# Row numbers cast once per batch, scatters behind a one-element GpSimd copy, z doubled by GpSimd, reciprocals taken in the expert tiles

## The chip, the core and the metric

The kernel runs on one core of one Trainium2 chip. The metric is the device time of one launch in microseconds (us). The profile is one execution recorded by the hardware profiler. Five engines work side by side: PE is TensorE (its weight loads are listed as PEld), DVE is VectorE, ACT is ScalarE, POOL is GpSimd, and SP is SyncE, which here only issues DMAs. GpSimd issues DMAs too, among them all indirect ones: a scatter that sends each of 128 rows to an address of its own.

## The reference

Two parts follow each other. The first is an attention without softmax that multiplies its result with u; the second is a dense feed-forward block to which each row adds the block of one expert out of eight, weighted with the softmax probability of that expert.

```python
# u, v: [8, 2816, 256]; z: [8, 2816, 64]
scores = (1.0 / S) * np.matmul(z, z.transpose(0, 2, 1))
attn = np.maximum(scores, 0.0) ** 2
x = (u * np.matmul(attn, v)).reshape(22528, 256)

y_dense = np.maximum(x @ w1_dense, 0.0) @ w2_dense        # 256 -> 512 -> 256
logits = x @ w_gate                                        # [22528, 8]
expert_idx = np.argmax(logits, axis=1)
gate_w = softmax(logits)[arange(N), expert_idx]
for e in range(8):
    mask = expert_idx == e
    y_moe[mask] = gate_w[mask, None] * (np.maximum(x[mask] @ w1[e], 0.0) @ w2[e])
return y_dense + y_moe
```

Since the largest logit is subtracted before the exponential, the chosen expert's probability is one divided by the sum of the exponentials. That is the only reciprocal in the kernel.

## The kernel before, in words

**Two stages.** The attention works through 176 row blocks of 128 rows, 22 in each of 8 batches. As soon as some row blocks have their x, they are routed: each row is given a place in the part of its expert in a buffer `xs` in DRAM, and a *scatter* sends it there, 576 bytes with x in bf16, the gate weight and the token's number. The expert stage reads `xs` back in tiles of 256 rows of one expert (70 of them) and then in pairs of 128 rows (22 of them, the last two only if they are needed), and sends the results to the output with indirect DMAs.

**The attention.** Row blocks are taken in groups of 2, 4, 4, 4, 4 and 4 per batch. For a group the scores against all 22 key blocks are computed on TensorE (L371), put through a ReLU by ScalarE (L386) or VectorE (L388) and squared by ScalarE (L399) or VectorE (L401; in the first two groups GpSimd may do it) into one of three buffers `A`. Since the scores are symmetric, part of A comes from the group before last by DMA transposes (L434). The products of A and v (`av`, L530) take two row blocks at a time in two passes over the 22 key blocks. `gate_x` (L559) multiplies with u and writes x to `pays`, a ring of 22 row blocks in SBUF, whose two last columns in use are the gate weight (column P, as float32) and the token number (column P + 1). Scores of up to two groups ahead fill TensorE's time in between.

**z.** For each batch, z is loaded (`load_z`), doubled along its columns by a copy in two halves (`turn_z`, L113), and transposed by SyncE's DMAs (L116). This is done during the batch before: the halves are due 6 and 7 row blocks after the batch's start, and the first scores that need them are computed from its fifth group on (row block 14).

**Routing.** Batches of row blocks are routed together: fourteen of 11, then 8, 6, 4 and 4 (`sizes`, L43), the first sixteen of them during the attention. `logits` (L587) multiplies with the gate's weights; `route_a` finds the largest logit, the exponentials `ex` and the one-hot `oh` of the chosen expert; `route_pre` counts on TensorE; the three parts of `route_b` write the gate weight (`se`, L634) and the token number (L635) to `pays` and work out the place of each row, a float32 number in `pos`. A batch is ready for scatters five row blocks and more after its last x.

**Scatters.** One is due at each *tick*, which comes once per row block (some 2.6 to 3.3 us). From row block 154 on, a second one is due in the middle of each pass. The last twelve are issued in the expert stage, one in each fifth slot (L1092 to L1095), with a `pause` behind it: a copy on GpSimd whose result is not read (L902). `scatter` casts one column of `pos` to an integer on VectorE (L675) and issues the indirect DMA on GpSimd (L677).

**What sets the order.** L67 gives a written order to four engines:

```python
    ctx.enter_context(tc.manual_schedule(engines={ET.PE, ET.Activation, ET.DVE, ET.SP}))
```

What is written first on one of these is issued first. A small planner makes this order while the kernel is built: work for VectorE or ScalarE is offered with a readiness time, a rank and an estimated duration per engine (`offer`), and `best` gives the engine that is free first the work that is ready first; TensorE's clock `now` is advanced by an estimate per piece of work (`pe`). The scatters are offered to VectorE with 0.1 us, because of their cast, and so are loads that are kept back by a small VectorE write (`soon`, rank 3; `turn_z` with 0.4 us). The routing's parts are offered with 1.3 us (`route_a`) and 0.8 us each (`chain`). GpSimd is not among the four: the framework that builds the program orders its instructions itself, within what their operands allow.

**The expert stage.** A slot computes, on TensorE, the dense block's first product, the second half's output of the tile two before, the expert's first product (L889) and the first half's output of the tile before (L897). VectorE copies the next tile's expert weights (L877). In `half` ScalarE copies the dense result out (L912), VectorE adds the expert's result times the row's gate weight (L913, the scalar `me[:, j, 0:1]` read back from `xs`), and GpSimd sends the 128 rows to the output (L915), with a `pause` behind every other one. `tokens` hands `half` the token numbers that came back with the rows.

## Time and profile before

| what | value |
|---|---|
| median of 3 runs | 939.89 us (938.05 to 944.79) |
| the profiled execution's own time | 936.83 us |
| its span | 934.7 us |
| mean granted TensorE clock | 0.99 |
| TensorE (PE) busy | 879.7 us, 94% |
| weight loads (PEld) busy | 762.7 us, 82% |
| VectorE (DVE) busy | 703.7 us, 75% |
| ScalarE (ACT) busy | 741.7 us, 79% |
| GpSimd (POOL) busy | 476.7 us, 51% |
| DMA | 127.64 MB, of these 61.54 MB read from HBM and 37.16 MB written |
| scatters to `xs` (L677) | 176, 199.2 us on GpSimd, mean 1132 ns |

The span runs from the first to the last recorded instruction. A busy time is the sum of an engine's recorded instructions; TensorE's matmuls are pipelined, so their ends are modelled. In the views that follow, `L677` is line 677 of the kernel, `xs<-pays,pi` names what an instruction writes and reads, and a time in brackets is the idle time of the engine ahead of an instruction with what ended it: `<-DVE pi L675` is an instruction of another engine, `<-issue` means that the profile shows nothing it waited for, and `<-remote` a release that the profile can't place. In the tables by stretches the engines stand in the order PE, PEld, DVE, ACT, POOL. A line of the waits reads: engine, tile and line that waited, what it waited for, total us, number of times, and the longest.

### The profile page before, as it was taken

What the parts mean: (1) busy time and instruction counts of PE and PEld (TensorE: products, weight loads), DVE (VectorE), ACT (ScalarE), POOL (GpSimd) and SP (SyncE); (2) the same over time, 40 slices, a digit from 0 to 9 for tenths busy, and PEclk for the clock granted to TensorE, in tenths of its full rate; (3) what the DMA queues carried; (4) which work ended last, traced back from release to release, by engine and by line L of the source; (5) the groups of instructions that cost most, each with busy time, mean ns of one, the idle gap of its engine ahead of it and who ended that gap; (6) DMA issues with size and microseconds to landing.
All of it is one profiled execution on the core that took longest, in us unless ns stands there. A gap on an engine that the chain in (4) does not pass through costs nothing.

```text
span 934.7 us, 30580 instructions
## 1 busy us (share of the span) xinstructions
PE 879.7 (94%) x12265; PEld 762.7 (82%) x12265; DVE 703.7 (75%) x1324; ACT 741.7 (79%) x916; POOL 476.7 (51%) x517
## 2 busy tenths in 40 slices
PE   7899999999999999999999988999999999999996
PEld 5788888888898898888888765878888888888775
DVE  7999988999898999999999873655654454446553
ACT  7999988999998999989989860666766676766664
POOL 2202342434344354344346334578877787876455
PEclk9999999999999999999999988999999999999999
DMA  7795896997997997997997845455544444443332
GB/s 146 119 177 124 150 177 134 158 195 147 157 191 152 172 196 142 177 198 139 182 181 150 132 105 88 108 120 114 119 111 112 109 113 109 117 103 95 85 88 70
DMA packets 257871, 127.64 MB, mean 137 GB/s; under 512 B 225470, under 2 KB 232894, under 8 KB 257728
## 3 DMA queue, kind: packets, MB, share of 16 engines
q1 hardware_dynamic: 230112, 70.24, 44.3%
q0 software_dynamic: 27616, 55.44, 27.8%
q8 instruction: 96, 1.57, 0.7%
q14 instruction: 47, 0.39, 0.2%
HBM read 61.54 MB, written 37.16 MB: 106 GB/s over the span
## 4 chain that ended last, share of the span: by engine, by line
PE 75%; issue 7%; DVE 5%; POOL 4%; ACT 4%; DMA 3%; another core or an unknown queue 1%; SPq 1%; POOLq 0%; DVEq 0%; ACTq 0%
PE o L530 38%; PE yy L897 13%; PE h_ps L889 12%; PE s L371 9%; POOL out_dram L915 3%; ACT A L399 2%; ACT r L386 1%; PE lg L587 1%; DVE A L401 1%; DMA xT<-pays 1%; DMA vb<-in_v_dram 1%; DVE ring L913 1%; DVE r L388 1%; ACT ring L912 1%
## 5 line engine op out<-in xcount | busy, mean ns | idle before, releaser
L530 PE MATMUL o<-vb,A 64*128 64x256 bf16 x7744 | 498.7, 271 | 12.3 <-issue 5.7
L530 PEld LDWEIGHTS <-A 64*128 64x128 bf16 x7744 | 411.1, 95 | 66.3 <-issue 12.4
L677 POOL DMA_INDIRECT xs<-pays,pi x176 | 199.2, 1132 | 274.3 <-DVE pi L675 224.9
L386 ACT ACTIVATE r<-s 128x1024 f32<-128x1024 f32 (+1 forms) x275 | 272.6, 1017 | 37.0 <-PE s L371 18.5
L399 ACT ACTIVATE A<-r 128x1024 bf16<-128x1024 f32 (+1 forms) x258 | 263.9, 1049 | 1.8 <-DVE vb L128 0.6
L892 ACT ACTIVATE ring<-h_ps 128x1024 bf16<-128x1024 f32 x180 | 185.6, 1032 | 95.1 <-PE yy L897 43.3
L401 DVE TENSOR_TENSOR A<-r 128x1024 bf16<-128x1024 f32 (+1 forms) x173 | 209.3, 1222 | 0.9
L913 DVE SCALAR_TENSOR_TENSOR ring<-yy,me,ring 128x256 f32<-128x256 f32 x180 | 86.3, 482 | 148.5 <-ACT ring L912 86.0
L388 DVE TENSOR_SCALAR r<-s 128x1024 f32<-128x1024 f32 x157 | 188.8, 1208 | 12.0 <-PE s L371 7.9
L915 POOL DMA_INDIRECT out_dram<-ring,me x140 | 145.9, 1042 | 63.7 <-DVE ring L913 34.2
L897 PEld LDWEIGHTS <-ring 128*128 128x128 bf16 x1440 | 140.0, 98 | 37.5 <-issue 21.4
L371 PE MATMUL s<-zT 64*128 64x512 bf16 (+1 forms) x944 | 159.4, 358 | 8.8 <-remote 3.8
L897 PE MATMUL yy<-w2d,ring 128*128 128x256 bf16 x720 | 107.9, 272 | 17.0 <-DVE ring L913 16.7
L897 PE MATMUL yy<-ring 128*128 128x256 bf16 x720 | 108.0, 273 | 0.0
L889 PE MATMUL h_ps<-ring 128*128 128x256 bf16 (+1 forms) x880 | 94.9, 253 | 1.7 <-issue 1.1
L889 PE MATMUL h_ps<-ring,w1d 128*128 128x256 bf16 x720 | 93.6, 273 | 2.6 <-ACT ring L892 1.2
L877 DVE COPY ring<-wall 128x2048 bf16 x110 | 81.9, 760 | 11.3 <-issue 8.4
L912 ACT COPY ring<-yy 128x256 f32<-128x256 f32 x180 | 68.1, 379 | 25.9 <-PE yy L897 12.2
L889 PEld LDWEIGHTS <-ring 128*128 128x128 bf16 x880 | 73.8, 98 | 11.4 <-DVE ring L877 2.3
L371 PEld LDWEIGHTS <-zT 64*128 64x128 bf16 x944 | 58.9, 94 | 25.3 <-issue 15.9
L889 PEld LDWEIGHTS <-w1d 128*128 128x128 bf16 x720 | 70.2, 98 | 11.3 <-issue 3.2
L559 DVE TENSOR_TENSOR pays<-o,ut 128x512 bf16<-128x512 f32 x88 | 60.7, 690 | 24.4 <-PE o L530 16.4
(118 smaller groups left out, 348.4 us busy)
## 6 DMA issues: line engine op xcount, KB each, us to landing
ut<-in_u_dram SPq DMA_DIRECT2D x88, 256.0 KB
vb<-in_v_dram POOLq DMA_DIRECT2D x16, 384.0 KB
vb<-in_v_dram POOLq DMA_DIRECT2D x16, 320.0 KB
wall<-in_moe_w_dram POOLq DMA_DIRECT2D x16, 256.0 KB
xs<-pays,pi POOLq DMA_INDIRECT x176
zr<-in_z_dram POOLq DMA_DIRECT2D x7, 352.0 KB
out_dram<-ring,me POOLq DMA_INDIRECT x140
A<-A SPq DMA_TRANSPOSE x128
```

What stands on the lines that cost most here:

```text
L371: nc.tensor.matmul(out=s[:, h, y * c:(y + 1) * c], lhsT=zT[r, k + h, :], rhs=zT[r, i0:i0 + w, :], start=True, stop=True)
L386: nc.scalar.activation(r[:, :, :c], s[:, :, :c], AF.Relu, scale=1.0 / S)
L388: nc.vector.tensor_scalar(out=r[:, :, :c], in0=s[:, :, :c], scalar1=1.0 / S, scalar2=0.0, op0=ALU.mult, op1=ALU.max)
L399: nc.scalar.activation(a, r, AF.Square)
L401: (nc.gpsimd if eng == "pool" else nc.vector).tensor_mul(a, r, r)
L530: nc.tensor.matmul(out=o[:, j, 0:D], lhsT=A[n][r, k, c:c + P], rhs=v_of[b][r, k, :], start=(p == 0 and x == 0), stop=(p == 1 and x == nK - 1))
L677: ins = nc.gpsimd.indirect_dma_start(out=xs, out_offset=bass.IndirectOffsetOnAxis(ap=pi[:], axis=0), in_=pays[:, g % (2 * G), 0:ROW].bitca ...
L889: nc.tensor.matmul(out=h_ps[:, f, hs, :], lhsT=w1(c, f), rhs=xT[:, hs, c, :], start=(c == 0), stop=(c == 1))
L892: nc.scalar.activation(h, h_ps[:].rearrange("p f h t -> p f (h t)"), AF.Relu)
L897: nc.tensor.matmul(out=y[:, k, :], lhsT=h[:, f, j * P:(j + 1) * P], rhs=w2(f), start=(f == 0), stop=(f == 3))
L913: nc.vector.scalar_tensor_tensor(out=ys, in0=y[:, 1, :], scalar=me[:, j, 0:1], in1=yd, op0=ALU.mult, op1=ALU.add)
L915: ins = nc.gpsimd.indirect_dma_start(out=out, out_offset=bass.IndirectOffsetOnAxis(ap=ids[j], axis=0), in_=ys, in_offset=None, bounds_chec ...
```

## The change

Six edits, of which the second and third belong together.

1. `turn_z`: the copy that doubles z is done by GpSimd and no longer by VectorE. It is no longer offered to the planner; it is written at its tick.
2. `route_b` part three casts the row numbers of a whole batch to integers at once (`pos`), and `scatter` hands a column of them to the indirect DMA. The 176 casts of one column each (L675) are gone.
3. A scatter is no longer offered to VectorE. At its tick a GpSimd copy of one element is written, from the piece of A that the planner gave last (`last_made`) to a one-element tile `pacer`, and the scatter behind it. The twelve scatters in the expert stage have no such copy.
4. The sum of the exponentials is written to `pays` as it is. The reciprocal is taken where the row comes back, in `tokens` of the expert stage: 128 x 2 numbers a tile (`mr`), which `half` uses as its scalar.
5. The token numbers are copied to `pays` by GpSimd; the one-hot is written in order and reads its input transposed, where it was the other way round.
6. The planner's durations follow: `route_a` 1.2 for 1.3, and `chain` 0.3, 0.55 and 0.8 for three times 0.8 (`1.05 - 0.25 * len(fns)`, with three, two and one part left).

```diff
--- before.py
+++ after.py
@@ -110,7 +110,7 @@
         if k0 == 0:
             zn_of[b] = zpool.tile([P, nK, 2, dq], BF, name="zn", bufs=1)
             zT_of[b] = zpool.tile([P, nK, P], BF, name="zT")
-        nc.vector.tensor_copy(
+        nc.gpsimd.tensor_copy(
             zn_of[b][:, k0:k1, :, :],
             z_of[b][:, k0:k1, :].unsqueeze(2).to_broadcast([P, k1 - k0, 2, dq]))
         nc.sync.dma_start_transpose(
@@ -403,6 +403,7 @@
         def done(t):
             r_free.append(t)
             r_free.sort()
+            last_made[:] = n, ks[0]
             for k in ks:
                 key_at[n, k] = key_at[n, k + 1] = t + 0.2
 
@@ -604,8 +605,8 @@
                                        op0=ALU.is_ge, op1=ALU.mult)
         nc.vector.tensor_reduce(out=m, in_=c, axis=AX.X, op=ALU.max)
         oh = vec("oh", E, n, BF)
-        nc.vector.tensor_tensor(out=oh.rearrange("p e t -> p t e"), in0=c,
-                                in1=bc(m), op=ALU.is_equal)
+        nc.vector.tensor_tensor(out=oh, in0=c.rearrange("p t e -> p e t"),
+                                in1=m.unsqueeze(1).to_broadcast([P, E, n]), op=ALU.is_equal)
         rs[q] = (oh, ex)
 
     made_first = [False]
@@ -627,12 +628,10 @@
         inc = vec("inc", E, n)
 
         def one():
-            se = vec("se", n)
-            nc.vector.tensor_reduce(out=se, in_=ex, axis=AX.X, op=ALU.add)
             o = starts[q] % (2 * G)
             rows = pays[:, o:o + n, :]
-            nc.vector.reciprocal(rows.bitcast(F32)[:, :, P], se)
-            nc.vector.tensor_copy(rows.bitcast(I32)[:, :, P + 1], tok[:, starts[q]:starts[q + 1]])
+            nc.vector.tensor_reduce(out=rows.bitcast(F32)[:, :, P], in_=ex, axis=AX.X, op=ALU.add)
+            nc.gpsimd.tensor_copy(rows.bitcast(I32)[:, :, P + 1], tok[:, starts[q]:starts[q + 1]])
             assert q != Q1 or made_first[0]
             if first_of[0] != n:
 
@@ -653,9 +652,11 @@
         def three():
             nc.vector.tensor_add(inc, inc, pre[1])
             nc.vector.tensor_mul(inc, inc, oh)
-            pos = vec("pos", n, bufs=3)
-            nc.vector.tensor_reduce(out=pos, in_=inc.rearrange("p e t -> p t e"),
+            row = vec("row", n)
+            nc.vector.tensor_reduce(out=row, in_=inc.rearrange("p e t -> p t e"),
                                     axis=AX.X, op=ALU.add)
+            pos = vec("pos", n, dt=I32, bufs=3)
+            nc.vector.tensor_copy(pos, row)
             rs[q] = pos
 
         return [one, two, three]
@@ -671,11 +672,9 @@
         q = max(q for q in range(nQ) if starts[q] <= g)
         j = g - starts[q]
 
-        pi = rt.tile([P, 1], I32, name="pi", bufs=16)
-        nc.vector.tensor_copy(pi[:], rs[q][:, j:j + 1])
         free["pool"] = max(free["pool"], now[0]) + 1.5
         ins = nc.gpsimd.indirect_dma_start(
-            out=xs, out_offset=bass.IndirectOffsetOnAxis(ap=pi[:], axis=0),
+            out=xs, out_offset=bass.IndirectOffsetOnAxis(ap=rs[q][:, j:j + 1], axis=0),
             in_=pays[:, g % (2 * G), 0:ROW].bitcast(F32), in_offset=None)
         if q < Q1:
             nodep(ins, ["xs"], "xs")
@@ -903,14 +902,14 @@
 
     def half(s, j):
 
-        hd, he, we, me, ids = pend[s]
+        hd, he, we, mr, ids = pend[s]
         we = we[j % len(we)]
         yd, ys = take("yd"), take("ys")
         y = late["y"].tile([P, 2, D], F32, name="yy", tag="y")
         down(y, 0, hd, lambda f: w2d[:, f, :], j)
         down(y, 1, he, lambda f: we[:, 2 * F + f * D:2 * F + (f + 1) * D], j)
         nc.scalar.copy(yd, y[:, 0, :])
-        nc.vector.scalar_tensor_tensor(out=ys, in0=y[:, 1, :], scalar=me[:, j, 0:1],
+        nc.vector.scalar_tensor_tensor(out=ys, in0=y[:, 1, :], scalar=mr[:, j:j + 1],
                                        in1=yd, op0=ALU.mult, op1=ALU.add)
         ins = nc.gpsimd.indirect_dma_start(
             out=out, out_offset=bass.IndirectOffsetOnAxis(ap=ids[j], axis=0),
@@ -921,12 +920,14 @@
 
     def tokens(s, me):
         mi = me[:].bitcast(I32)
+        mr = mx.tile([P, 2], F32, name="mr")
+        nc.vector.reciprocal(mr[:], me[:, :, 0])
         if s < NT1:
-            return [mi[:, j, 1:2] for j in range(2)]
+            return mr, [mi[:, j, 1:2] for j in range(2)]
         ix = mx.tile([P, 2], I32, name="ix")
         nc.vector.tensor_tensor(out=ix[:], in0=mi[:, :, 1], in1=inv[:, 2 * (s - NT1):2 * (s - NT1) + 2],
                                 op=ALU.bitwise_or)
-        return [ix[:, j:j + 1] for j in range(2)]
+        return mr, [ix[:, j:j + 1] for j in range(2)]
 
     MAYBE = 2
     AHEAD = 9
@@ -952,7 +953,7 @@
             half(0, 0)
         if s < end:
             he = up(xT, [lambda c, f, w=w: w[:, c * F + f * P:c * F + (f + 1) * P] for w in we])
-            pend[s] = (hd, he, we, me, tokens(s, me))
+            pend[s] = (hd, he, we) + tokens(s, me)
         if s > 1 and s - 1 in pend:
             half(s - 1, 0)
 
@@ -975,8 +976,8 @@
         t = b * nK
         if b + 1 < B:
             soon(t + 1, lambda b=b: load_z(b + 1))
-            soon(t + 6, lambda b=b: turn_z(b + 1, 0, nK // 2), 0.4)
-            soon(t + 7, lambda b=b: turn_z(b + 1, nK // 2, nK), 0.4)
+            at(t + 6, lambda b=b: turn_z(b + 1, 0, nK // 2))
+            at(t + 7, lambda b=b: turn_z(b + 1, nK // 2, nK))
             for h in range(4):
                 soon(t + 10 + 2 * h, lambda b=b, h=h: load_v(b + 1, h, 4))
 
@@ -988,16 +989,18 @@
             soon(ts.pop(0), lambda e=e, part=part: weights(e, part))
     waiting = []
     placed = set()
-
-    def one_scatter(dve=True):
+    pacer = const.tile([1, 1], BF, name="pacer")
+    last_made = [0, 0]
+
+    def one_scatter(pace=True):
         if not waiting:
             return
         g = waiting.pop(0)
-        if dve:
-            offer(now[0], 0, {"dve": (0.1, lambda eng: scatter(g))}, lambda t: placed.add(g))
-        else:
-            scatter(g)
-            placed.add(g)
+        if pace:
+            n, k = last_made
+            nc.gpsimd.tensor_copy(pacer[:], A[n][0:1, k, 0:1])
+        scatter(g)
+        placed.add(g)
 
     routed = []
 
@@ -1009,14 +1012,14 @@
             else:
                 then(t)
 
-        offer(t, 0.5, {"dve": (0.8, lambda eng: fns[0]())}, done)
+        offer(t, 0.5, {"dve": (1.05 - 0.25 * len(fns), lambda eng: fns[0]())}, done)
 
     def routing(q):
         def first():
             bank_of[q] = take_pair()
             logits(q)
             now[0] += 0.6
-            offer(now[0] + 0.2, 0, {"dve": (1.3, lambda eng: route_a(q))}, middle)
+            offer(now[0] + 0.2, 0, {"dve": (1.2, lambda eng: route_a(q))}, middle)
 
         def middle(t):
             give_pair(t, bank_of[q])
@@ -1091,7 +1094,7 @@
             fn()
         if s % 5 == 1 and waiting:
             g = waiting[0]
-            one_scatter(dve=False)
+            one_scatter(pace=False)
             pause(pays[:, g % (2 * G), 0:ROW].bitcast(F32))
     assert not waiting
     assert not later
```

## The prediction

> **What bounds the kernel now.** I read the page, then busy time by stretches, then who waited for whom, then the order of time on GpSimd and TensorE. The attention fills the first 585 us, the expert tiles the rest. By stretches (start and end, length, then busy time with instruction counts, granted clock, DMA share, GB/s):
>
> ```profile
> span 934.7 us, 30580 instructions
> 100.00:500.00 400.00, 394.31 (x6660) 343.58 (x6656) 372.23 (x667) 368.38 (x400) 170.66 (x171) 1.00 0.99 168
> 508.00:518.00 10.00, 7.86 (x121) 6.03 (x117) 6.41 (x12) 6.77 (x8) 6.17 (x6) 1.00 0.96 167
> 531.00:544.00 13.00, 8.43 (x127) 6.85 (x124) 9.46 (x27) 7.27 (x9) 7.99 (x7) 0.85 0.96 183
> 544.00:561.00 17.00, 17.00 (x271) 14.26 (x268) 14.15 (x32) 14.85 (x18) 5.38 (x4) 0.92 0.38 79
> 561.00:574.00 13.00, 9.10 (x139) 6.46 (x134) 2.81 (x11) 1.88 (x2) 8.38 (x8) 0.87 0.57 98
> 574.00:585.00 11.00, 10.12 (x150) 7.97 (x148) 5.87 (x24) 0.24 (x1) 2.65 (x3) 0.84 0.50 78
> 585.00:934.70 349.70, 322.14 (x3056) 283.23 (x3053) 181.40 (x387) 230.51 (x362) 245.08 (x275) 1.00 0.44 105
> ```
>
> From 100 to 500 us TensorE is busy 394.31 of 400 us (98.6%) while VectorE has 27.8 us free and ScalarE 31.6. TensorE bounds this stretch, and what VectorE saves there is mostly not on the path. What TensorE waited for in 25 to 505 us, as far as VectorE and ScalarE are named with over 0.5 us (total, times, longest; the PEld rows are the weight loads):
>
> ```profile
> PE o L530 <- DVE A L401: 1.5, 3, 0.7
> PE o L530 <- ACT A L399: 0.8, 1, 0.8
> ...
> PEld L530 <- DVE A L401: 2.6, 3, 1.1
> ...
> PEld L530 <- ACT A L399: 1.6, 2, 1.2
> ```
>
> That is 6.5 us at most, partly counted twice. The other three short stretches are different: TensorE stands there, and each time GpSimd is issuing indirect scatters one behind the other. GpSimd in order of time, first where the attention runs undisturbed, then in such a run, and TensorE in the two worst runs:
>
> ```profile
> 304.25 0.99 POOL L677 DMA_INDIRECT xs<-pays,pi  x1 [2.15 <-DVE pi L675]
> 305.55 0.58 POOL L106 DMA_DIRECT2D zr<-in_z_dram  x1 [0.30 <-issue]
> 306.83 0.99 POOL L677 DMA_INDIRECT xs<-pays,pi  x1 [0.70 <-DVE pi L675]
> 310.01 0.96 POOL L677 DMA_INDIRECT xs<-pays,pi  x1 [2.19 <-DVE pi L675]
> ```
> ```profile
> 561.88 1.76 POOL L677 DMA_INDIRECT xs<-pays,pi  x1 [9.88 <-DVE pi L675]
> 563.95 0.97 POOL L677 DMA_INDIRECT xs<-pays,pi  x1 [0.31 <-issue]
> 565.22 0.97 POOL L677 DMA_INDIRECT xs<-pays,pi  x1 [0.30 <-issue]
> ...
> 570.31 0.96 POOL L677 DMA_INDIRECT xs<-pays,pi  x1 [0.30 <-issue]
> ```
> ```profile
> 542.98 0.61 PE L371 MATMUL s<-zT 64*128 64x512 bf16 x2 [3.82 <-remote]
> ```
> ```profile
> 569.76 0.30 PE L530 MATMUL o<-vb,A 64*128 64x256 bf16 x2 [1.15 <-issue]
> 571.22 0.40 PE L530 MATMUL o<-vb,A 64*128 64x256 bf16 x2 [1.15 <-issue]
> ```
>
> In the quiet stretch scatters start some 2.6 us apart, each behind its own VectorE cast. From 563.95 to 570.31 six start every 1.27 us, and near their end TensorE issues two matmuls in 1.5 us with no wait that the profile can name. The other two runs are five scatters from 509 and seven from 531 us. What a run does to the other engines the trace does not say; that it does something it says three times.
>
> **The price of a run.** At 98.6% the three short stretches would have 9.86, 12.82 and 12.82 us of TensorE work; they have 7.86, 8.43 and 9.10, so 2.0 + 4.4 + 3.7 = 10.1 us are lost. The clock is 0.92 in the 17 us and 0.84 in the 11 us behind the last two: 1.4 + 1.8 = 3.1 us more. Together 13.2 us for three runs of 5, 7 and 7: 4.4 us a run, or 0.69 us a scatter.
>
> [...]
>
> **The change, part by part.** (1) The 176 casts of L675 go, and with them the wait by which VectorE's order held each scatter back:
>
> ```profile
> POOL xs L677 <- DVE pi L675: 224.9, 117, 9.9
> ```
>
> GpSimd stood 224.9 us for them. In their place the row numbers of a batch are cast once, and a one-element GpSimd copy that reads the newest piece of A is written ahead of each scatter. What orders GpSimd? L67 gives a written order to TensorE, ScalarE, VectorE and SyncE; GpSimd is missing, so the framework lays out its instructions by when it reckons their inputs are there. The trace shows that this can turn the written order round. L1094 to L1096 write a scatter and behind it a copy of the row that it sends; on the chip the copy comes first, because the scatter's cast was late:
>
> ```profile
> 590.88 0.31 POOL L902 COPY zr<-pays 128x144 f32<-128x144 f32 x1
> 591.88 0.99 POOL L677 DMA_INDIRECT xs<-pays,pi  x1 [0.69 <-DVE pi L675]
> ```
>
> After the change all eleven scatters of a batch have their inputs as soon as the one cast is done, and nothing they read is written by the pacer. The pacers of later ticks wait for pieces of A that come 2.6 us apart. So the later scatters are laid out ahead of their pacers, and GpSimd issues a batch in one run: eleven at 1.27 us (0.97 + 0.30), or 2.0 us where one takes 1.7, some 14 to 18 us instead of 29. This is my main choice.
>
> There are then 18 runs (14 of 11, then 8, 6, 4, 4; L43) where there were three. At 4.4 us a run, the two of four at half, 17 x 4.4 = 74.8 us, less the 13.2 present: +62. At 0.69 a scatter, 176 x 0.69 - 13.2 = +108. The runs seen stand in a stretch with less VectorE work; where the square of L401 runs beside a scatter it is longer (1.76 at 561.88 against 0.97) and the run looser, so I take +70, near the lower. The lowest is that of a loose run: in the expert tiles eighteen scatters go out from 790.77 to 819.03, 1.66 us apart, and TensorE keeps going:
>
> ```profile
> 790.77 1.28 POOL L915 DMA_INDIRECT out_dram<-ring,me  x1 [1.72 <-DVE ring L913]
> ...
> 819.03 0.98 POOL L915 DMA_INDIRECT out_dram<-ring,me  x1 [0.17 <-issue]
> ```
> ```profile
> 790.00:820.00 30.00, 28.82 (x263) 25.62 (x263) 14.85 (x27) 21.59 (x33) 24.40 (x27) 1.00 0.46 109
> ```
>
> There 30 us hold 28.82 us of TensorE work, more than the 92% of the whole stage, so such runs cost next to nothing.
>
> (2) VectorE's other savings, by shape (busy us, mean ns of one, idle before; below, GpSimd's copies with min/median/max):
>
> ```profile
> L675 DVE CAST pi<-pos 128x1 int32<-128x1 f32 x176 | 26.1, 154 | 0.2
> L113 DVE COPY zn<-zr 128x1408 bf16<-128x1408 bf16 x14 | 11.9, 878 | 0.0
> L607 DVE TENSOR_TENSOR oh<-c,m 128x88 bf16<-128x88 f32 x14 | 7.8, 560 | 0.5
> L655 DVE TENSOR_TENSOR inc<-inc,oh 128x88 f32<-128x88 f32 x14 | 3.5, 253 | 0.5
> L634 DVE RECIPROCAL pays<-se 128x11 f32<-128x11 f32 x14 | 3.2, 228 | 0.5
> L635 DVE COPY pays<-tok 128x11 int32<-128x11 int32 x14 | 2.0, 140 | 0.0
> L634 DVE RECIPROCAL pays<-se 128x4 f32<-128x4 f32 x2 | 0.4, 180 | 0.1
> ```
> ```profile
> L902 POOL COPY zr<-ring x70: 411/434/941, 590.4 to 853.0; 128x256 f32<-128x256 f32 x70
> L902 POOL COPY zr<-pays x12: 306/316/650, 590.9 to 801.7; 128x144 f32<-128x144 f32 x12
> ```
>
> The casts (26.1), the doubling of z (11.9), the old reciprocals (3.2) and the token copies (2.0) leave VectorE; the one-hot, written in order now, should cost between L655's 253 ns and its own 560, so up to 4.3 less; 18 batch casts at about 154 come back (2.8). That is 40 to 45 us of VectorE, nearly all beside a busy TensorE. It is worth at most the 6.5 us above; I take -3, ends 0 and -7. The planner's new durations for VectorE shuffle who takes which square; I give that nothing, with 2 us either way.
>
> (3) On GpSimd the z copy: from 316 ns for 144 and 434 for 256 elements, 1.05 ns an element, so 0.32 + 1264 x 1.05 ns = 1.65 us, 14 times 23 us. The pacers, about 0.2 us each from the same line, up to 164 times: 33 us. GpSimd has 229 of 400 us free. SyncE's z transposes (L116) now wait for GpSimd; behind them on SyncE stand u loads (L144), A transposes (L434) and x transposes (L561). A copy that gets in behind a run could hold them some 14 us; the scores of a batch are computed up to two groups of rows ahead, so z is first read some seven row blocks (about 20 us) after the second copy, and u rows are fetched four blocks ahead, so I price it at nothing, and up to 2 us for each of 7 batches in the upper end.
>
> ```profile
> PE yy L897 <- DVE ring L913: 16.7, 23, 1.9
> ```
>
> (4) The 90 reciprocals in the expert tiles take about 180 ns (the 128x4 row): 16 us of VectorE, which is busy 181 of 350 us there. They stand in VectorE's queue behind the weight copies and ahead of the second combine of a slot; when that is late, TensorE waits for its bank. Ends 0 and 4 us (the 23 such waits above by 0.18); I take +2.
>
> **Sum.** 936.8 us (the profiled execution; the median of the runs shown is 939.9) + 70 - 3 + 2 = 1006 us. With the ends of the run price, 936.8 + 8 = 945 and 936.8 + 108 + 4 = 1049, or 1063 with SyncE held up.
>
> **Rivals.** *The pacers hold* (not slower): GpSimd's layout keeps pacer and scatter paired. The place is GpSimd's queue; it decides if, within a batch, scatters start over 2 us apart. For it: the copies are short and their pieces of A recent. Against: the turned pair above. Then only -3 + 2 remain, and the two late runs may dissolve: 936 us, or 926 if 10 of the 13.2 us go.
>
> *Loose runs*: the layout is lost, but L401 spreads the runs to 1.6 us and they cost as at 790 us: 176 x 0.05 = +8, 945 us. Against: the run from 531 starts as loosely (1.95, 1.82, 1.53 us) and loses 4.4.
>
> *The z copy blocks VectorE*: the scatter at 561.88 lasts 1.76 us beside L401, which takes both inputs from SBUF, so the two engines stand in each other's way. If the 14 copies stop VectorE in turn, it loses 23 of the 43 us that it gained: about 939 us, with the pacers holding. [...]
>
> **How the numbers follow.** Tight runs 0.57 (most of it between 945 and 1050), loose runs 0.12, pacers hold 0.28 with or without the z block, something else 0.03. Of the 0.28, 0.15 is faster by over 1%, which is about what a measurement here can tell from no change; of the loose runs 0.07 stay within it, and of the tight ones 0.01. So faster 0.15, same 0.21, slower 0.64. The range 925 to 1050 holds the forecast's case and the pacing one down to its lower figure; 945 to 1050 is the likeliest case alone.
>
> **What the profile after would show.** Right: scatters of a batch 1.3 to 2 us apart from the first batch on, pacers bunched behind them, TensorE's busy share in 100 to 500 us down from 98.6% to about 88%, with stops named "issue" or "remote" and stretches of clock under 1. Wrong: scatters still 2.6 us apart behind a GpSimd copy, or tight runs beside a TensorE that goes on. The z step is right if L116 waits for GpSimd under 2 us each; the reciprocals if waits for L913 stay near 17 us.

## The result, and the profile after

The changed kernel takes 1058.34 us (median of 6 runs, 1044.4 to 1063.11); the kernel before took 941.05 us beside it (6 runs, 934.39 to 945.81). The ratio is 1.122, with a 95% interval of 1.116 to 1.128; runs over 1.5% above the fastest of their kernel are left out of the ratios. The profiled execution took 1056.81 us, 120.0 us more than that of before.

The page of the changed kernel, its span, TensorE's and GpSimd's line, and the granted clock in 40 slices:

```profile
span 1055.1 us, 30759 instructions
...
PE 931.7 (88%) x12267; PEld 782.3 (74%) x12267; DVE 711.6 (67%) x1218; ACT 736.3 (70%) x904; POOL 549.1 (52%) x713
...
PEclk9898989899898898999989899888899999999999
```

TensorE does the same work in 931.7 us instead of 879.7, and stands still for 123.4 us instead of 55.0. So of the 120.4 us by which the span grew, 68.4 are time in which TensorE did nothing and 52.0 are time by which the same work took longer. Most of the 52.0 is the clock: by the trace's clock record 90.1 us of TensorE's work ran at half clock, against 12.8 us in before, and half of the difference is 38.6 us. The clock row has an 8 in every second or third slice of the attention, where it had two in all.

Where the time went is told by the hand-over from the attention to the expert tiles. TensorE in order of time, first of before, then of after:

```profile
584.32 1.03 PE L889 MATMUL h_ps<-ring,w1d 128*128 128x256 bf16 x8 [0.79 <-DVE pays L559]
```
```profile
700.95 1.03 PE L888 MATMUL h_ps<-ring,w1d 128*128 128x256 bf16 x8 [0.80 <-DVE pays L560]
```

The attention ends 116.6 us later; the expert tiles, 350.4 us before, take 354.2. Busy time by stretches of the changed kernel (columns as in the prediction):

```profile
100.00:500.00 400.00, 338.50 (x5168) 275.65 (x5168) 295.36 (x405) 283.96 (x304) 175.38 (x254) 0.91 0.75 130
...
701.00:1055.10 354.10, 326.11 (x3060) 286.88 (x3059) 186.87 (x464) 231.71 (x362) 248.71 (x277) 0.98 0.43 104
```

In the 400 us in which before issued 6660 matmuls, the changed kernel issues 5168. GpSimd in order of time, in the routing batch from 126 us:

```profile
126.92 1.72 POOL L676 DMA_INDIRECT xs<-pays,pos  x1 [2.19 <-DVE pos L659]
128.95 1.38 POOL L676 DMA_INDIRECT xs<-pays,pos  x1 [0.31 <-issue]
130.63 0.96 POOL L676 DMA_INDIRECT xs<-pays,pos  x1 [0.30 <-issue]
131.60 0.18 POOL L1001 COPY pacer<-A 1x1 bf16<-1x1 bf16 x1
131.93 0.98 POOL L676 DMA_INDIRECT xs<-pays,pos  x1 [0.15 <-issue]
...
140.81 0.96 POOL L676 DMA_INDIRECT xs<-pays,pos  x1 [0.30 <-issue]
141.77 0.42 POOL L1001 COPY pacer<-A 1x1 bf16<-1x1 bf16 x2
```

The first scatter waits for the one cast (`pos`, L659), the other ten follow without a wait for anything that the profile shows, from 131.93 on every 1.27 us, and the pacers that were written ahead of them are issued behind. What such a run does to the others is plainest in the next batch, whose scatters go out from 173.34 to 189.08 us. By stretches:

```profile
165.00:185.00 20.00, 19.38 (x317) 16.30 (x314) 16.26 (x28) 15.93 (x19) 10.79 (x11) 1.00 0.57 119
185.00:191.70 6.70, 0.00 (x0) 0.00 (x0) 0.41 (x1) 1.06 (x1) 4.80 (x9) 0.70 0.58 152
191.70:194.60 2.90, 2.87 (x24) 2.04 (x25) 2.45 (x2) 2.23 (x3) 0.00 (x0) 0.51 0.01 0
194.60:205.00 10.40, 10.40 (x177) 9.41 (x175) 9.33 (x11) 9.19 (x10) 1.72 (x4) 1.00 0.91 78
205.00:215.00 10.00, 8.26 (x142) 6.41 (x140) 8.07 (x12) 7.33 (x10) 4.13 (x6) 1.00 1.20 128
```

For 6.70 us TensorE issues nothing, and VectorE and ScalarE finish one instruction each; only GpSimd goes on. Behind the stop the clock is 0.51 for 2.90 us, and TensorE, busy nearly all of them, gets through 24 matmuls, 120 ns each, where at full clock it did 317 in 19.38 us, 61 ns each; then the clock is 1.00 again.

It is TensorE that stops, and the other two wait for it. VectorE's square at 184.18 takes 1.23 us and ScalarE's at 185.09 takes 1.06, near the means of 1.24 and 1.05 of their squares of this size in the whole span. Their next instructions come late:

```profile
191.75 1.23 DVE L388 TENSOR_SCALAR r<-s 128x1024 f32<-128x1024 f32 x1 [6.34 <-remote]
192.38 1.02 ACT L386 ACTIVATE r<-s 128x1024 f32<-128x1024 f32 x1 [6.23 <-PE s L371]
```

The page can't place the first release, but the trace's semaphore records can: the semaphore on which TensorE, VectorE and ScalarE all wait here is raised by TensorE's instructions alone. Three matmuls that raise it begin from 184.37 to 184.55, and the records have it raised at 191.65, 191.69 and 191.73, with nothing between. The full stops that end at 101.65, 231.75, 368.16, 457.48 and 541.69 show the same. So TensorE's last matmuls before a full stop are begun but report 4 to 7 us late, within 3 us of the end of the run (here its last scatter ends at 190.04). Whether the matmuls are held or only their report, these records don't tell.

The waits of TensorE from 100 to 500 us sum this up; before had neither line there:

```profile
PE o L531 <- issue: 28.3, 46, 1.5
PE s L371 <- remote: 24.7, 5, 6.8
```

The second line is the full stop. The first is a slow one, in which TensorE gets three matmuls out every 1.43 us, with no wait that the profile can name:

```profile
357.88 0.38 PE L531 MATMUL o<-vb,A 64*128 64x256 bf16 x3 [1.06 <-issue]
...
359.31 0.38 PE L531 MATMUL o<-vb,A 64*128 64x256 bf16 x3 [1.06 <-issue]
```

### The profile page after: what moved, and what is told of

It reads as the page before. It is cut to its first block, busy times and chain, and to the rows that moved or that the text cites. A ratio compares the mean times of both kernels' runs of the same rounds, so it can differ in the third digit from the quotient of the medians.

```text
span 1055.1 us, 30759 instructions
## 1 busy us (share of the span) xinstructions
PE 931.7 (88%) x12267; PEld 782.3 (74%) x12267; DVE 711.6 (67%) x1218; ACT 736.3 (70%) x904; POOL 549.1 (52%) x713
## 4 chain that ended last, share of the span: by engine, by line
PE 50%; issue 6%; DVE 5%; POOL 4%; another core or an unknown queue 3%; ACT 2%; DMA 1%; POOLq 0%; DVEq 0%; ACTq 0%
PE o L531 22%; PE yy L896 11%; PE h_ps L888 11%; PE s L371 5%; POOL out_dram L914 3%; DVE A L401 1%; DVE r L388 1%; ACT r L386 1%; POOL zr L901 1%; DVE ring L912 1%; DVE pays L560 1%; ACT ring L891 1%; ACT ring L911 1%; DMA xT<-pays 0%
## 5 line engine op out<-in xcount | busy, mean ns | idle before, releaser
L531 PE MATMUL o<-vb,A 64*128 64x256 bf16 x7744 | 538.7, 279 | 36.6 <-issue 31.8
L531 PEld LDWEIGHTS <-A 64*128 64x128 bf16 x7744 | 426.1, 97 | 121.1 <-issue 64.2
L386 ACT ACTIVATE r<-s 128x1024 f32<-128x1024 f32 (+1 forms) x271 | 268.1, 1009 | 150.8 <-PE s L371 74.1
L399 ACT ACTIVATE A<-r 128x1024 bf16<-128x1024 f32 (+1 forms) x250 | 255.9, 1041 | 10.4 <-DVE r L388 7.8
L388 DVE TENSOR_SCALAR r<-s 128x1024 f32<-128x1024 f32 x161 | 194.7, 1220 | 90.3 <-PE s L371 41.3
L676 POOL DMA_INDIRECT xs<-pays,pos x176 | 200.1, 1137 | 103.9 <-DVE pos L659 51.2
L401 DVE TENSOR_TENSOR A<-r 128x1024 bf16<-128x1024 f32 x181 | 221.8, 1241 | 6.6 <-ACT r L386 3.7
L371 PE MATMUL s<-zT 64*128 64x512 bf16 (+1 forms) x944 | 170.1, 376 | 48.0 <-remote 33.8
L912 DVE SCALAR_TENSOR_TENSOR ring<-yy,mr,ring 128x256 f32<-128x256 f32 x180 | 86.3, 481 | 147.7 <-ACT ring L911 74.0
L1001 POOL COPY pacer<-A 1x1 bf16<-1x1 bf16 x164 | 43.4, 265 | 97.2 <-DVE A L401 50.6
```

The lines of the kernel that those rows point to most:

```text
L371: nc.tensor.matmul(out=s[:, h, y * c:(y + 1) * c], lhsT=zT[r, k + h, :], rhs=zT[r, i0:i0 + w, :], start=True, stop=True)
L386: nc.scalar.activation(r[:, :, :c], s[:, :, :c], AF.Relu, scale=1.0 / S)
L388: nc.vector.tensor_scalar(out=r[:, :, :c], in0=s[:, :, :c], scalar1=1.0 / S, scalar2=0.0, op0=ALU.mult, op1=ALU.max)
L399: nc.scalar.activation(a, r, AF.Square)
L401: (nc.gpsimd if eng == "pool" else nc.vector).tensor_mul(a, r, r)
L531: nc.tensor.matmul(out=o[:, j, 0:D], lhsT=A[n][r, k, c:c + P], rhs=v_of[b][r, k, :], start=(p == 0 and x == 0), stop=(p == 1 and x == nK - 1))
```

## The experiments

Each runs beside the kernel before on the same chip. "Pinned" means that the framework is told to keep a scatter behind the pacer written ahead of it; it puts no wait into the program.

**One: the pacers made to hold.**

```diff
+        if pinned:
+            tc.keep_in_program_order(ins)
```

> The changed kernel with every scatter of the attention pinned in GpSimd's order behind its own pacer; nothing else differs. If the runs of eleven are the whole loss (theory), scatters start over 2 us apart, the stops of TensorE go, and the time is what the rival 'the pacers hold' gave: 926 to 937 us. If another edit carries part of the loss (z doubled by GpSimd, the token copy on GpSimd, the reciprocals in the expert tiles, each written outside the scatters), it stays: over 950 us.

Measured: 962.59 us (4 runs, 961.31 to 965.3), ratio 1.025 (1.018 to 1.032). GpSimd in order of time now has the pairs, and by stretches TensorE is back near its load:

```profile
409.45 0.18 POOL L1003 COPY pacer<-A 1x1 bf16<-1x1 bf16 x1 [1.20 <-ACT A L399]
410.15 0.99 POOL L676 DMA_INDIRECT xs<-pays,pos  x1 [0.51 <-issue]
412.95 0.18 POOL L1003 COPY pacer<-A 1x1 bf16<-1x1 bf16 x1 [1.80 <-DVE A L401]
413.63 1.76 POOL L676 DMA_INDIRECT xs<-pays,pos  x1 [0.51 <-issue]
```
```profile
100.00:500.00 400.00, 383.82 (x6411) 332.43 (x6408) 362.02 (x501) 348.78 (x378) 220.27 (x311) 0.99 0.94 162
```

This one line of order, which adds no instruction and no wait, takes 96 us back from 1058.34. TensorE's full stops shrink with it, from 24.7 to 7.0 us in this stretch, the longest from 6.8 to 1.8. The rest of the expectation failed: the time is 26 us over its upper end, so something else, in the change or in pacing that holds, costs about 2.5%.

**Two: no pacers at all.** `scatter(g)` alone, the copy left out.

> The changed kernel without the one-element copies; the scatters are free. Theory (the runs cost, the pacers are bystanders behind them): the runs stay as they are, 1045 to 1065 us. Rival (the overtaken pacers, which pile up behind a run and wait for A, hold up the token copy, z and v on GpSimd's queue): at least 15 us faster than the changed kernel, under 1042 us.

Measured: 1054.96 us, and 1072.73, which is left out; one run gives no interval. It lies within the range expected of bystanders, 3 us under the changed kernel. The pacers, where they are overtaken, neither help nor harm by as much as can be seen here.

**Three: the cast alone.**

```diff
-        pi = rt.tile([P, 1], I32, name="pi", bufs=16)
-        nc.vector.tensor_copy(pi[:], rs[q][:, j:j + 1])
...
+            pos = vec("pos", n, dt=I32, bufs=3)
+            nc.vector.tensor_copy(pos, row)
```

> The kernel before with one edit: the row numbers cast once per batch, the 176 single casts gone. No pacer, z, token numbers and reciprocals as before. Theory: GpSimd sends each batch in one run, eighteen runs, and the time is that of the changed kernel, 1040 to 1065 us. Rival (the loss comes from an edit that is not in this kernel): under 960 us.

Measured: 1063.8 us (2 runs), ratio 1.132 (1.121 to 1.143). As expected, one edit of six makes a loss as large as all six together: with the single casts gone, nothing ties a scatter to VectorE's order any more.

**Four, thirteen and fourteen: runs of four, two and six.** A pacer ahead of every fourth (second, sixth) scatter of a batch, with the scatters up to the next one pinned behind it:

```diff
-        if pace:
+        if pace and (g % G % 4 == 0 or last_p[0] is None):
             n, k = last_made
-            nc.gpsimd.tensor_copy(pacer[:], A[n][0:1, k, 0:1])
+            last_p[0] = nc.gpsimd.tensor_copy(pacer[:], A[n][0:1, k, 0:1])
...
+            behind(ins, last_p[0])
```

> Like the kernel with every scatter pinned, but a pacer only ahead of every fourth scatter of a batch and its four scatters pinned behind it: runs of 4, 4 and 3. If each scatter in a tight run costs the same (about 0.8 us by the changed kernel's 120 us over 164 scatters), the loss stays, over 1020 us. If a run costs nothing until some 6 us after its start, as the first stops of TensorE in the changed kernel suggest (96.4 for the run from 87.5, 132.6 for the one from 126.9), runs of four, 5 us long, are free: within 10 us of the kernel with every scatter pinned.

> The pinned kernel with a pacer ahead of every second scatter and two scatters behind it. By the stops of TensorE counted so far (mean 1.3 us in a run of three or four, 4.8 us in a run of eleven) the stops begin with the third scatter, and runs of two are as good as single ones: 955 to 972 us. If each scatter in a tight pair costs like one in a run of four (55 us over the pinned kernel): over 985 us.

> The same with runs of six and five. If the price of a run grows with the time that it lasts after its first two or three scatters, the sum lies between runs of four (1018 us) and of eleven (1058 to 1064 us): 1020 to 1050 us. If what counts is the number of runs, not their length, it is less than with runs of four: under 1005 us.

Measured: two 972.41 us (964.63, and 980.19, which is left out below), four 1017.97 us (ratio 1.083, 1.072 to 1.095), six 1038.28 us (1.105, 1.093 to 1.118). By stretches, and the waits of TensorE there, for two, four and six in turn:

```profile
100.00:500.00 400.00, 376.42 (x6289) 324.79 (x6290) 355.77 (x494) 343.29 (x370) 196.18 (x251) 1.00 0.94 160
```
```profile
PE o L531 <- issue: 1.1, 4, 0.3
```
```profile
100.00:500.00 400.00, 357.48 (x5730) 298.32 (x5730) 321.84 (x449) 311.00 (x336) 173.45 (x198) 0.98 0.83 143
```
```profile
PE s L371 <- remote: 15.3, 7, 3.9
PE o L531 <- issue: 8.7, 22, 1.0
```
```profile
100.00:500.00 400.00, 354.84 (x5517) 292.59 (x5513) 310.32 (x435) 298.05 (x322) 168.03 (x182) 0.95 0.79 139
```
```profile
PE o L531 <- issue: 20.5, 40, 1.2
PE s L371 <- remote: 9.8, 3, 5.1
```

The slow stops go 1.1, 8.7, 20.5 and 28.3 us for runs of two, four, six and eleven. The full stops don't grow as evenly: 15.3 us for four, 9.8 for six, 24.7 for eleven. The runs of six came as the first of their two expectations had it. Neither expectation of the runs of four held as it stood: they are not free, and the sum isn't that of a fixed price for each scatter, which would give the same total for all lengths. What fits all three longer ones is a price for each scatter after the second of its run. The 164 scatters of the attention (176 less the twelve of the expert stage) are 45 runs by fours, 30 by sixes and 16 by whole batches, so 74, 104 and 132 come after a second one; over the pinned kernel's 962.6 us the losses are 55, 76 and 96 us, which is 0.75, 0.73 and 0.73 us each. For runs of two this rule gives nothing, and the 964.63 is 2 us over the pinned kernel, one run alone. The scatters are counted here from the edits; on the chip some runs break up, and the pinned kernel has a few bunches of five left, so the price is an estimate from four kernels and not the reading of one stop.

**Five, nine and ten: what the paced kernel still loses.** In the pinned kernel GpSimd waits for z and the token copy with scatters behind it. Five takes both back to VectorE; ten is five with the planner's durations of before (1.3 and 0.8 us); nine is the kernel before with the batch cast and pinned pacers alone, offered to the planner as the casts were:

```diff
-            offer(now[0], 0, {"dve": (0.1, lambda eng: scatter(g))}, ...)
+            offer(now[0], 0, {"dve": (0.1, lambda eng: paced(g))}, ...)
```

> The kernel with every scatter pinned behind its pacer, and the doubling of z and the copy of the token numbers back on VectorE. In the pinned kernel (962.6 us) the scatters bunch to five or six at 1.3 to 1.9 us behind GpSimd's waits for the token copy (5.92 us at 212.02) and for z (3.94 us at 250.13). If these waits make what is left of the loss, the bunches go and the time is 930 to 945 us. If the pacers' own ties to A make it, it stays over 955 us.

> The kernel before with the batch cast and a pacer with its scatter pinned behind it, offered to the planner with 0.1 us of VectorE as the single casts were; z, token numbers, reciprocals, one-hot and the planner's durations as before. The two pinned versions of the changed kernel are 2.5% slower than before. If the planner's new durations or the other edits make that, this kernel is at 925 to 942 us. If the pacers make it (each holds a buffer of A until GpSimd has read it, and waits for A with other work behind it), it stays at 950 to 965 us.

> The pinned kernel with z and token numbers on VectorE (955.9 us), and the planner's durations of the routing as before (1.3 and 0.8 us). If the new durations carry the rest of the loss: under 945 us. If the pacers do, or the scatters that are no longer offered to the planner: 950 to 962 us.

Measured: five 955.87 us, ratio 1.025 (1.023 to 1.028); ten 962.01 us, 1.020 (1.009 to 1.030); nine 951.36 us, 1.011 (1.001 to 1.021). In five no more than three scatters stand close together before the last eight, and the ratio is the pinned kernel's, so the bunches behind GpSimd's waits are not the cause, nor are the durations. Batch cast and pacers alone are no gain and probably a loss of about 1%:

```profile
100.00:500.00 400.00, 391.23 (x6600) 341.10 (x6597) 365.42 (x548) 365.78 (x396) 201.06 (x295) 1.00 0.98 168
```

Nine issues 6600 matmuls in the stretch, sixty fewer than before, beside a VectorE with less to do. Where the other 1.4% come from isn't settled: the intervals of nine and ten overlap, and the edits that remain cost nothing alone (below). Ten differs from nine in the one-hot, the reciprocals and in that scatters are written at their tick and not offered; these were not taken apart.

All the paced kernels share one more thing, as does the changed kernel: at the hand-over the runs are still there. The last eight paced scatters find the last pieces of A made, so nothing holds them back (nine: 569.21 to 578.47, 1.32 us apart), and the twelve of the expert stage have neither a cast of their own nor a pacer: six go out in one run from 591.33 to 598.21 and the others by 624.09, where before sends one some 19 us after the other. The first 36.5 us of the expert stage, of before and of nine:

```profile
583.50:620.00 36.50, 34.13 (x324) 30.16 (x323) 20.41 (x59) 22.43 (x35) 23.87 (x29) 1.00 0.51 112
591.80:628.30 36.50, 24.49 (x212) 20.22 (x213) 14.70 (x50) 15.16 (x23) 23.70 (x27) 0.91 0.49 107
```

TensorE does 10 us less there (the pinned kernel, five and ten do 24.8 to 26.1 us of work). The rest of the stage gets about half of it back: from the attention's last product on, nine takes 356.6 us, before 351.2. So part of what the paced kernels lose may be such runs and not the pacing. No run here holds the last scatters back, so this is not shown.

**Six and seven: two edits by themselves.** The kernel before with z doubled by GpSimd, and the kernel before with the reciprocals in the expert tiles.

> The kernel before with one edit: z doubled by GpSimd, written at its tick. Scatters keep their VectorE casts. Theory: GpSimd waits for z's load with scatters behind it, which come out in a bunch of three or four: 0 to 10 us over the kernel before. [...]

> The kernel before with one edit: the sums of exponentials stored, the reciprocals taken in the expert tiles. The prediction's step had 0 to 4 us, +2 taken; the changed kernel's expert stage is 3.8 us longer (355.0 against 351.2 us from the last product of the attention). Expected: +1 to +4 us. If the longer expert stage has another cause (the clock), within 1 us.

Measured: 929.95 us, ratio 0.998 (0.995 to 1.001), and 933.23 us, ratio 1.000 (0.997 to 1.003). Both are free, and neither is worth anything.

**Eight: runs of eleven, but slower.** No pacer; ahead of each scatter four short GpSimd writes that wait for nothing, all pinned in a row:

```diff
-            nc.gpsimd.tensor_copy(pacer[:], A[n][0:1, k, 0:1])
+            for x in range(4):
+                prev, last_p[0] = last_p[0], nc.gpsimd.memset(rest[:], 0.0)
```

> The changed kernel without pacers, each scatter instead pinned behind four short GpSimd writes that wait for nothing: a batch still goes out in one run of eleven, but at 2.2 to 2.6 us a scatter and no longer at 1.27. If the rate of scatters makes the loss: 940 to 975 us. If their number in a row makes it, or GpSimd being busy without a break: over 1020 us.

Measured: 1013.93 us (2 runs), ratio 1.087 (1.081 to 1.094), which is between the two expectations. GpSimd in order of time, and TensorE's waits over the whole span:

```profile
290.13 0.97 POOL L684 DMA_INDIRECT xs<-pays,pos  x1 [0.16 <-issue]
...
291.09 1.65 POOL L1012 MEMSET rest<- 128x320 bf16 x4
...
292.90 0.97 POOL L684 DMA_INDIRECT xs<-pays,pos  x1 [0.16 <-issue]
```
```profile
PE o L531 <- DMA vb<-in_v_dram: 36.1, 21, 6.8
PE h_ps L899 <- DVE pays L560: 18.8, 1, 18.8
PE s L371 <- DVE r L388: 7.6, 9, 2.7
PE s L371 <- ACT r L386: 4.7, 4, 2.4
```

At 2.8 us a scatter the attention's stops named issue and remote are gone (from 100 to 500 us TensorE has none), though GpSimd is hardly idle in a run. The loss is another one: v's loads stand behind the run in GpSimd's queue and come late (36.1 us), and the last batches too (18.8 us). Those two are 54.9 of the 81 us by which the median exceeds that of before beside it (933.08). What makes the other 26 us was not followed. So the stops go with the rate of the scatters, and not with eleven in a row or with a GpSimd that takes no break; but the run shows too why a pause of fixed length is no pacing.

**Eleven and twelve: GpSimd busy without scatters.** The kernel before, and beside it for each batch a run of eleven plain DMAs of the same rows to a spare buffer (eleven), or 55 small multiplications (twelve):

```diff
+                nc.gpsimd.dma_start(out=scr[g * P:(g + 1) * P, :], in_=pays[:, g % (2 * G), 0:ROW].bitcast(F32))
```
```diff
+                    nc.gpsimd.tensor_tensor(out=rest[:], in0=ones[:, 0:1].to_broadcast([P, 192]), ...)
```

> The kernel before, and beside it for each batch eleven plain DMAs issued by GpSimd in one run, each 128 rows of 576 bytes from the same ring to a buffer in DRAM that nobody reads. If any row-wise DMA that GpSimd issues in a tight run stops TensorE: fourteen and more runs at some 7 us each, over 1020 us, with waits of the products named issue. If it takes the indirect form: under 960 us.

> The kernel before, and beside it for each batch 55 small GpSimd multiplications (128x192) whose result is not read, 12 to 20 us of GpSimd work without a break and without a DMA. If a busy GpSimd as such stops TensorE: over 1000 us. If it takes scatters: under 965 us, with no waits of the products named issue; what is lost then is work that comes late behind GpSimd.

Measured: eleven 970.71 us (2 runs), ratio 1.033 (1.020 to 1.046); twelve 1336.68 us (2 runs), 1.42. Eleven lies between its two expectations. For the plain DMAs, GpSimd in order of time and TensorE's waits from 100 to 500 us:

```profile
152.19 4.30 POOL L1037 DMA_DIRECT2D scr<-pays  x8 [1.15 <-DVE pays L636]
```
```profile
PE s L372 <- remote: 8.5, 3, 3.7
...
PE o L531 <- issue: 0.7, 3, 0.3
```

They go out every 0.54 us, twice as fast as the scatters, and the slow stop of TensorE isn't there (0.7 us against 28.3). The three full stops, 8.5 us, were not followed further, and neither was the rest of the 3%. The multiplications overloaded GpSimd: 597 ns each, 55 of them 33 us for a batch that comes every 29. The page's groups, and VectorE's waits:

```profile
L1038 POOL TENSOR_TENSOR rest<-ones,pos 128x192 bf16<-128x192 bf16 x840 | 501.9, 597 | 86.3 <-DVE pos L657 24.1
L530 PE MATMUL o<-vb,A 64*128 64x256 bf16 x7744 | 527.2, 281 | 13.4 <-issue 6.8
```
```profile
DVE pays L559 <- DMA xs<-pays,pi: 311.2, 27, 26.2
```

The scatters come so late that VectorE waits 311.2 us for free rows in `pays`. So the time is over the 1000 us of the first expectation, but not by its mechanism. As a price that says nothing; as a sign it does, since the products wait 6.8 us for "issue", as in before (5.7), beside a GpSimd that computes for 501.9 us more.

**Fifteen: before with fewer late scatters.** The second scatter of a pass only while row blocks below 154 wait, and one in three expert slots instead of five.

> The kernel before with its late runs loosened: the second scatter of a pass is issued only while row blocks below 154 wait, and the expert stage takes one scatter in three slots, not five. Three scatters move. If the three late runs of before (13 us) are shortened by that: 3 to 8 us under before; if other scatters close up in their place: no change.

Measured: 941.12 us, ratio 1.000 (0.996 to 1.005). Nothing is gained by moving three scatters; whether the 13 us of before's late runs can be had is open. No version here beats the kernel before.

## Why the prediction was right and wrong

**Right: the bound, the order, the mechanism.** TensorE bounds the attention; VectorE's savings bought nothing that can be seen (six, seven and nine are within 0.2% of before or slower). GpSimd's instructions were laid out as the turned pair at 590.88 and 591.88 said: scatters in one run, pacers behind. The sign that was named, tight runs from the first batch on with stops called issue or remote and a clock under 1, is what the profile shows; TensorE's share in 100 to 500 us fell to 84.6% (338.50 of 400), where 88% was forecast.

**Wrong: the size, in the step "The price of a run".** The forecast was +69 us, and 1050 the upper end; measured are +117 (the profiled executions differ by 120). The step took 4.4 us a run "near the lower" of two prices. Per run of the changed kernel's sixteen in the attention, the 116.6 us are 7.3. The mis-sized term has two parts. First, the price grows with the length of the run: about 0.73 us for each scatter after the second fits the runs of four, six and eleven. The three runs that set the price, of five, seven and seven, have 13 such scatters, so their 13.2 us are 1.0 us each; a run of eleven has nine. So a price of runs with three to five of them was used for runs that have mostly nine. The other end, 0.69 us for every scatter less the 13.2 us present, gave +108, which is near the measured +117 by luck: it prices the first two of a run like the rest, which the runs of two speak against. It was passed over because the runs seen stood beside less VectorE work. Second, the clock: in before it was 3.1 of 13.2 us, while in the changed kernel it is 38.6 of the 120.4 us of the span, from 23% to 32%. After 184.93 TensorE stands, at some 187.7, 2.8 us into the stop, the clock halves (0.70 is the mean of the 6.70 us), and it stays at half until 2.90 us after the work goes on (the row at 191.70). In before, by its clock record, it is at half from 540.0, 0.9 us into the stop of 3.82 us that ends at 542.98, to 546.9, and from 570.8 to 577.6 at the end of the run from 561.

The 0.73 us a scatter do not close the account. Pinned, the kernel has few of these runs left in the attention and is still 2.5% over before. What makes that part stays open; the runs at the hand-over, named under nine, are one candidate.

**Small terms.** Measured against the working (a line of the groups each, by shape, of the changed kernel, then its waits):

```profile
L924 DVE RECIPROCAL mr<-me 128x2 f32<-128x2 f32 x90 | 13.9, 155 | 0.0
L608 DVE TENSOR_TENSOR oh<-c,m 128x88 bf16<-128x88 f32 x14 | 5.1, 364 | 0.5
```
```profile
L113 POOL COPY zn<-zr 128x1408 bf16<-128x1408 bf16 x14 | 23.5, 1701 | 41.2 <-DMA zr<-in_z_dram 41.2
L1001 POOL COPY pacer<-A 1x1 bf16<-1x1 bf16 x164 | 43.4, 265 | 97.2 <-DVE A L401 50.6 <-ACT A L399 43.3 <-POOL pacer L1001 0.2
```
```profile
PE yy L896 <- DVE ring L912: 14.0, 13, 3.9
```

The reciprocals are 155 ns (180 taken) and make no wait of TensorE longer (14.0 us, 17 at most expected); alone they cost nothing, so the +2 was 0. The one-hot is 364 ns, within 253 to 560. z's copy is 1.70 us by GpSimd against 1.65 worked out, and it waits 41.2 us for z's load, which costs nothing that can be seen (six); the profile names no wait of SyncE's transposes of z (L116) for GpSimd. The pacers take 265 ns, not 200.

**The rivals.** "The pacers hold" failed in its condition, and its price was wrong too: made to hold, they give 962.6 us, not 926 to 936. "Loose runs" failed: in the run from 126.92 the first two scatters take 1.72 and 1.38 us, but from 131.93 on they come every 1.27. "The z copy blocks VectorE" failed in its price. The two do stand in each other's way: in before 33 of the 91 scatters that overlap a square of L401 take over 1.5 us, and none of the 39 that overlap L388 alone takes over 1.01; in the changed kernel five of the eight squares beside a z copy take 1.78 to 2.52 us, and none of the 172 others of their size over 1.23. But that is 4.4 us of VectorE's time and not 23, and with z doubled by GpSimd alone the ratio is 0.998 (six).

## What to carry to other kernels

An instruction that only paces must be tied to what it paces: where the framework orders an engine by readiness, a wait written ahead of ready work is simply overtaken, and a small cast on a slow-moving engine may be the pacing that nobody wrote down. Price a disturbance by its size, not by its count: when the runs that you can see are shorter than those that the change makes, take the price per unit, and add the clock that each stop costs behind it (here 38.6 of 120.4 us in all). And before a wait is removed from an engine that has time to spare, ask what the wait held back; what it saved here (VectorE's 40 us) lay from the start beside a TensorE that was the bound.

## What the runs showed of the hardware that was not expected

Indirect scatters that GpSimd issues every 1.27 us hold TensorE up, to three matmuls in 1.43 us and then to a full stop of up to 6.79 us. ScalarE and VectorE are not held: what they have runs at about its usual length (1.06 and 1.23 us at 185.09 and 184.18, by means of 1.05 and 1.24), and then they wait for TensorE. With the clock's share a run costs an estimated 0.73 us for each scatter after the second of a run, by runs of four, six and eleven over the pinned kernel. At 2.8 us apart there are no such stops from 100 to 500 us (eight); plain DMAs of the same rows at 0.54 us apart bring no slow stop, 0.7 us, though three full stops of 8.5 us in all (eleven); and GpSimd computing for 501.9 us more brings no slow stop either, 6.8 us against 5.7 (twelve). The amount of DMA traffic is no explanation: the transfers of 185.00 to 191.70 are a share of 0.58, under the 0.99 of before's undisturbed stretch. By which path the scatters hold up TensorE no run here shows; that its matmuls report late, near the end of the run, is as far as the traces go.
